# Moving x sums and Sinkhorn steps around the end of the first expert, in a fused attention and mixture-of-experts kernel

## The chip, the cores and the metric

The kernel runs on one core of a Trainium2 chip. The metric is the device time of one execution in microseconds. Shown are the median of several executions and one further execution taken with the hardware profiler, whose page and trace are quoted below. The engines are TensorE (PE: matmuls, with its weight loads listed as PEld), VectorE (DVE), ScalarE (ACT), GpSimd (POOL) and SyncE (SP), which here only issues DMAs.

## The reference

```python
# attention: batch 8, heads 8, seq 576, head_dim 64; result x is 4608 tokens x 512
q_p, k_p = phi(q), phi(k)                     # relu, times cos and sin of the position
x = (q_p @ (k_p.T @ v)) / (q_p @ sum(k_p) + 1e-6)
# mixture of experts: D = 512, E = 8 experts, F = 1024
P = exp(x @ w_gate - max)                     # 4608 x 8
for _ in range(8):                            # Sinkhorn
    P /= P.sum(1, keepdims=True) + 1e-9
    P /= P.sum(0, keepdims=True) + 1e-9
    P *= N / E
out = sum over e of P[:, e:e+1] * (relu(x @ w1[e]) @ w2[e])
```

The routing is dense: every token goes through every expert, and only the weights `P` depend on the Sinkhorn loop. `P` depends on all tokens, so it cannot be complete before the attention of the last batch is.

## The kernel before, in words

**First part, blocks 0 to 6.** A block is 512 tokens, and one loop turn per block has 16 slots. In slots 0 to 7 TensorE computes one of the eight 128-column pieces of expert 0's first layer (`ffn1`, four matmuls of 512 columns) and ScalarE applies the relu. In slots 8 to 15 it computes the second layer of the block's four 128-token tiles (`ffn2`), two slots a tile, and the tile is copied from PSUM into the accumulator `acc`. Between the slots the attention of the next batch is dealt out from a table (`at(block, slot, function)`). `xT` holds x with the feature on the partitions.

**Second part, blocks 7 and 8 and unit 0.** After block 6 the attention pools are given back and their memory is used again by `wB` (expert 1's weights), `H`, `S1/S2/S4`, `T...` and others. Blocks 7 and 8 are the last 1024 tokens of expert 0. Experts 1 to 7 are computed by a scheme of Strassen's kind with seven products in place of eight. It takes 384 tokens from the first half of all tokens and 384 from the second as a *unit*; there are six units an expert. A unit's first layer has four *groups* (`group`) of seven products, each of two matmuls of 384 columns. The products need sums of x parts, made by `x_sums(n, ts)`: four VectorE instructions, three into tiles `S1, S2, S4` and one in place in `xT`. The three are also saved to DRAM (`x_saved`), and later experts load them again (`x_again`). They also need sums of weights (`w1_steps`, sixteen VectorE instructions for one expert). The second layer is done by `Pair`, seven products of four matmuls of 256 columns for each pair of tiles; `stream` deals it into the fills of the next unit.

Each group calls `fill()` seven times. In unit 0 of expert 1 the fill is `start_fill`, in all later units `pair_fill`. Fill number k of unit 0 is therefore 7 x group + place. `start_fill` deals out the second layer of block 8 (`tiles`, from `dealt`) and steps of Sinkhorn.

**Sinkhorn** is the generator `sinkhorn()`, eight iterations of five steps: row sums and their reciprocal (`rs`, `rr`); the scaling and the column sums over a partition's tokens (`colp`); up to two weight steps; a TensorE matmul with ones that sums `colp` over the partitions into the bank `W2`, and the rest of the weight steps; the reciprocal of that and the second scaling of `P_tok`. `balanced(n)` takes n steps. Sinkhorn and the units meet on TensorE and VectorE only.

**Order.** `te, ve, se` (the tuple `bound`) are wrappers that add to each instruction an ordering dependency on the one before it on its engine, so that it runs in written order. From unit 1 on `ve` is the plain engine, and from expert 2 on `se` is, so that there the framework's scheduler chooses the order when the program is built. In the trace wrapped instructions have line 109, plain ones their own line. `gate(g)` multiplies a finished tile of expert 0 by its weight `P_tok[:, g, 0:1]`; two of the 36 go to GpSimd, and 34 to ScalarE, six a unit through units 1 to 5 and the last four in the first unit of expert 2.

Of the kernel before, what the change touches and what calls it, by code (L numbers as in the profile page):

```python
# [11 lines left out]
F16 = mybir.dt.float16  # L12

AX = mybir.AxisListType
ALU = mybir.AluOpType
# [10 lines left out]
def kernel(  # L26
# [10 lines left out]
    nc = tc.nc  # L37
# [117 lines left out]
    def ffn2(hT, w, c0, g, y_ps, fts):  # L155

        for ft in fts:
            te.matmul(
                out=y_ps,
                lhsT=hT[:, ft, c0 : c0 + P],  # L160
                rhs=w[1][:, ft, :],
                start=(ft == 0),
                stop=(ft == FT - 1),
            )
        if FT - 1 in fts:

            if g % 2 == 0 or g < (B - 1) * TCH // P:
                se.copy(out=acc(g), in_=y_ps)
            else:
                ve.tensor_copy(out=acc(g), in_=y_ps)  # L170

    def store(g, cols=slice(0, Dm), queues=(nc.sync, nc.sync)):
        for half, queue in enumerate(queues):
            w_ = 2 * g + half
            b, c = w_ // C, w_ % C
            rows = out[b * S : (b + 1) * S].rearrange("(p c) d -> p c d", c=C)
            queue.dma_start(
                out=rows[:, c, cols], in_=acc(g)[half * HP : (half + 1) * HP, cols]
            )

    with ExitStack() as p1:
        ld = p1.enter_context(tc.tile_pool(name="ld", bufs=4))
# [485 lines left out]
        for j in range(B):  # L668
# [82 lines left out]
            if j == 1:  # L751
                for name in "qkv":
                    for half in range(2):
                        at(j, 12, load, b + 2, half, name, True)
            elif j and b + 2 < B:
                for half in range(2):
                    at(j, 11 + half, load, b + 2, half, "qkv", True)
        y_pss = {}
        for j in range(B - 1):
            if j:  # L760
# [34 lines left out]

    NT = N // 2
    TU = 3 * P
    NU = NT // TU  # L800
    KH = KT // 2
    FH = FT // 2
    UG = TU // P
    DH = Dm // 2
    w_next = load_weights(wB, 1)

    H = hB.tile([P, 2, FT, 2 * TU], F16, name="H")
# [12 lines left out]
    Y = ps_k.tile([P, TCH], FP32, name="copied_ps")  # L820
    Z = ps_k.tile([P, TCH], FP32, name="p7_ps")

    def x_part(half, kh, n):
        t0 = half * NT + n * TU
        return xT[:, kh * KH : (kh + 1) * KH, t0 : t0 + TU]

    x_saved = dram.tile([NU, 3, P, KH * TU], F16, name="x_saved")

    def x_tiles():
        return [s2_pool.tile([P, KH, TU], F16, name=name) for name in ("S1", "S2", "S4")]  # L830

    def x_sums(n, ts):

        a11, a12, a21, a22 = (x_part(i, j, n) for i in range(2) for j in range(2))
        s1, s2, s4 = (t[:] for t in ts)
        for out_, in0, in1, op in (
            (s1, a21, a22, ALU.add), (s2, s1, a11, ALU.subtract),
            (s4, a12, s2, ALU.subtract), (a21, a11, a21, ALU.subtract),
        ):
            ve.tensor_tensor(out=out_, in0=in0, in1=in1, op=op)  # L840
            yield
        for i, t in enumerate(ts):
            nc.sync.dma_start(out=x_saved[n, i], in_=t[:].rearrange("p k t -> p (k t)"))
# [260 lines left out]
    def gate(g, pool=None):  # L1104

        if pool is None:
            se.mul(out=acc(g), in_=acc(g), mul=P_tok[:, g, 0:1])
# [43 lines left out]


    OFFSETS = {"P1": 0, "P2": 3, "P7": 4, "P6": 5, "P4": 8, "P5": 9, "P3": 13}
# [21 lines left out]
    def start_fill():  # L1175

        nonlocal k_fill
        if k_fill % 7 in (0, 2, 3, 5):
            next(tiles, None)
        if k_fill % 6 != 1:  # L1180
            balanced(1)
        k_fill += 1

    def pair_fill():
        nonlocal k_fill, slot2
        k_fill += 1
        if k_fill % 4 and stream and stream[0][0] <= slot2:
            _, pair, name = stream.pop(0)
            pair.step(name)
        if (k_fill % 7 == 6 or k_fill % 7 == 4 and k_fill % 4 in (1, 2)) and ungated:  # L1190

            gate(ungated.pop(0))
        slot2 += bool(k_fill % 4)

    mark(Y[:])
    for e in range(1, E):
# [3 lines left out]
        for n in range(NU):  # L1200
            hT = next_h()
            xs = xs_next
            for i in range(FH):
                group(hT, tws[i], xs, n, i, start_fill if e == 1 and n == 0 else pair_fill)
                m = (n + 1) % NU
                if e == 1 and m:

                    if n == 0:
                        xs_next = xs_first[1]
                        continue  # L1210
                    if i == 0:
                        xs_next = x_tiles()
                        sums_x = x_sums(m, xs_next)
                    next(sums_x)
                    if i == FH - 1:
                        next(sums_x, None)
                elif i == 1:
                    xs_next = x_tiles()
                    if not (e == E - 1 and m == 0):
                        x_again(m, xs_next)  # L1220
# [61 lines left out]
```

The softmax here doesn't subtract the row's maximum and nothing guards it: scores larger than these inputs give would overflow.

## Time and profile before

| what | value |
|---|---|
| median of 8 runs | 978.61 us (977.5 to 980.76) |
| the profiled execution | 978.05 us |
| its span, first to last instruction | 976.3 us |
| TensorE busy | 961.4 us, 98% of the span |
| VectorE busy | 807.5 us, 83% |
| ScalarE busy | 564.0 us, 58% |
| granted TensorE clock | 0.999 |

The rows of the timeline give start, duration, engine, line, operation and operands, and in brackets how long the engine sat idle before the instruction, with the engine that released it. A matmul row gathers several matmuls (x2 is one product of a group). The end of a matmul is modelled, and it overlaps the next one: the time that a product takes of TensorE is the distance from its start to the next start, 0.33 us for two matmuls of 384 columns and 0.22 us for one of 512. On VectorE and ScalarE too, the next instruction can start before the listed end of the one before.

The stretch that the change touches goes from block 6 (from 143.6 us) to the start of unit 1 (206.2 us). From there to the end TensorE works on units 1 to 41 of the seven experts, 18.3 to 18.6 us each.

### The profile page before, as it was taken

Reading aid. Unit: us, or ns where it says so; the run is one execution under the profiler, and the core shown is the slowest. Engines: PE = TensorE matmul, PEld = TensorE weight load, DVE = VectorE, ACT = ScalarE, POOL = GpSimd, SP = SyncE. Lnnn points to the kernel's source line nnn. Section 1 sums busy time; section 2 is a strip of 40 time slices with the busy share of each in tenths; the row PEclk is TensorE's granted clock in tenths of the full one; section 3 lists DMA queues with packets and bytes.
Section 4 is the critical chain, followed back from the end, with each engine's and each line's share of the span. In section 5 each row is a group of like instructions: output and inputs, shape, how many; then the busy total and the mean of one; then the engine's idle time right before and its main releaser. Section 6 shows DMA issues by size and latency. Waiting matters only on the chain.

```text
span 976.3 us, 20236 instructions
## 1 busy us (share of the span) xinstructions
PE 961.4 (98%) x7855; PEld 674.5 (69%) x7855; DVE 807.5 (83%) x1833; ACT 564.0 (58%) x1262; POOL 60.7 (6%) x82
## 2 busy tenths in 40 slices
PE   9999999999999999999999999999999999999997
PEld 6545555457777777777777777777777777777775
DVE  7767775888988987987888987988888888988887
ACT  5766665477776555555555555555555555555551
POOL 6231110010000000000000000000000000000001
PEclk9999999999999999999999999999999999999999
DMA  9999986330104401323103401323103401104435
GB/s 162 185 153 174 152 141 111 68 68 34 42 26 84 77 25 42 67 53 66 33 26 85 77 25 42 65 53 66 35 26 81 80 25 40 35 26 122 126 89 128
DMA packets 80336, 73.54 MB, mean 75 GB/s; under 512 B 33264, under 2 KB 72176, under 8 KB 80240
## 3 DMA queue, kind: packets, MB, share of 16 engines
q0 software_dynamic: 27232, 30.94, 20.4%
q1 hardware_dynamic: 52768, 41.06, 17.2%
q8 instruction: 61, 1.00, 0.4%
q14 instruction: 35, 0.29, 0.1%
q10 hardware_dynamic: 240, 0.26, 0.1%
HBM read 83.12 MB, written 12.98 MB: 98 GB/s over the span
## 4 chain that ended last, share of the span: by engine, by line
PE 88%; DMA 5%; DVE 3%; issue 2%; ACT 1%; POOL 1%; POOLq 0%; ACTq 0%; SPq 0%
PE rows_ps L109 33%; PE h_ps L109 26%; PE p_ps L109 11%; PE copied_ps L109 11%; PE y_ps L109 4%; PE small_ps L109 2%; DMA k_ld<-in_k_dram 1%; DMA w1e<-in_moe_w_dram 1%; DMA w2e<-in_moe_w_dram 1%; DMA acc_hi<-q_p 1%; DVE P_tok L109 1%; DVE colp L109 0%; POOL q_ld L202 0%; DVE rs L109 0%; DVE acc_hi L955 0%
## 5 line engine op out<-in xcount | busy, mean ns | idle before, releaser
L955 DVE SCALAR_TENSOR_TENSOR acc_lo<-rows_ps,P_tok,acc_lo 128x512 f32<-128x512 f32 (+1 forms) x322 | 203.1, 639 | 74.9 <-PE rows_ps L109 74.9
L109 PEld LDWEIGHTS <-H 128*128 128x128 f16 x2080 | 203.1, 98 | 82.5 <-issue 1.2
L891 ACT CAST u<-h_ps 128x384 f16<-128x384 f32 x288 | 137.8, 478 | 131.1 <-PE h_ps L109 131.1
L109 PEld LDWEIGHTS <-w1e 128*128 128x128 f16 x1632 | 157.7, 98 | 67.6 <-issue 5.2
L885 DVE CUSTOM_DVE_ANT_0 H<-p_ps,u 128x384 f16<-128x384 f32 x329 | 180.9, 550 | 6.6 <-PE p_ps L109 6.6
L109 PEld LDWEIGHTS <-hs 128*128 128x128 f16 x1500 | 146.6, 98 | 56.2
L109 PE MATMUL h_ps<-S,w1e 128*128 128x384 f16 x672 | 164.1, 326 | 0.7 <-ACT u L109 0.6
L109 PE MATMUL p_ps<-xT,T 128*128 128x384 f16 x672 | 164.1, 326 | 0.1
L109 PE MATMUL rows_ps<-V,H 128*128 128x256 f16 x1000 | 150.0, 273 | 0.7 <-DVE acc_hi L955 0.7
L109 PE MATMUL rows_ps<-w2e,hs 128*128 128x256 f16 x1000 | 150.0, 273 | 0.0
L109 PE MATMUL h_ps<-xT,w1e 128*128 128x384 f16 (+1 forms) x616 | 148.7, 350 | 0.1
L923 ACT ACTIVATE H<-h_ps 128x384 f16<-128x384 f32 x144 | 70.7, 491 | 95.0 <-PE h_ps L109 95.0
L109 PEld LDWEIGHTS <-T 128*128 128x128 f16 x1008 | 98.4, 98 | 30.1 <-issue 3.5
L109 PE MATMUL rows_ps<-w2e,H 128*128 128x256 f16 (+1 forms) x568 | 92.3, 285 | 0.0
L904 ACT COPY copied_ps<-h_ps 128x384 f32<-128x384 f32 x144 | 67.5, 469 | 35.4 <-PE h_ps L109 35.4
L914 ACT ACTIVATE H<-copied_ps 128x384 f16<-128x384 f32 x144 | 70.9, 492 | 20.3 <-PE copied_ps L109 20.3
L109 PE MATMUL h_ps<-S,T 128*128 128x384 f16 x336 | 81.8, 325 | 0.4 <-ACT copied_ps L109 0.3
L109 PE MATMUL copied_ps<-xT,w1e 128*128 128x384 f16 x336 | 82.1, 326 | 0.0
L109 PE MATMUL copied_ps<-w2e,H 128*128 128x256 f16 x504 | 75.5, 272 | 0.0
L109 PE MATMUL rows_ps<-V,hs 128*128 128x256 f16 x500 | 75.0, 272 | 0.0
L955 DVE SCALAR_TENSOR_TENSOR acc_lo<-copied_ps,P_tok,acc_lo 128x256 f32<-128x256 f32 x126 | 60.0, 476 | 0.6 <-PE copied_ps L109 0.2
L955 DVE SCALAR_TENSOR_TENSOR acc_hi<-rows_ps,P_tok,acc_hi 128x512 f32<-128x512 f32 (+1 forms) x56 | 41.2, 736 | 20.5 <-PE rows_ps L109 19.7
(145 smaller groups left out, 946.6 us busy)
## 6 DMA issues: line engine op xcount, KB each, us to landing
S<-x_saved SPq DMA_DIRECT2D x108, 192.0 KB, 2.4
out_dram<-acc_lo SPq DMA_DIRECT2D x62, 128.0 KB, 2.4
w1e<-in_moe_w_dram POOLq DMA_DIRECT2D x7, 1024.0 KB, 8.7
w2e<-in_moe_w_dram POOLq DMA_DIRECT2D x7, 1024.0 KB, 9.8
q_ld<-in_q_dram POOLq DMA_DIRECT2D x16, 288.0 KB, 6.6
k_ld<-in_k_dram POOLq DMA_DIRECT2D x16, 288.0 KB, 8.0
v_ld<-in_v_dram POOLq DMA_DIRECT2D x16, 288.0 KB, 9.2
x_saved<-S SPq DMA_DIRECT2D x18, 192.0 KB, 1.9
```

Of the source, the lines that this page charges most:

```text
L109: i = getattr(self.engine, name)(*args, **kwargs)
L885: latest = ve._custom_dve(TENSOR_ADD_SAT, out=out, in0=ps[:, 0:TU], in1=t[:], s0=FP32_MAX, s1=0.0)
L891: se.copy(out=t[:], in_=ps[:, 0:TU])
L904: se.copy(out=Y[:, 0:TU], in_=X[:, 0:TU])
L914: se.activation(out=h11, in_=Y[:, 0:TU], func=AF.Relu)
L923: se.activation(out=h12, in_=X[:, 0:TU], func=AF.Relu)
L955: ve.scalar_tensor_tensor(out=a, in0=rows, scalar=P_tok[:, g, self.e : self.e + 1], in1=a, op0=ALU.mult, op1=ALU.add,)
```

## The change

It has five parts.

1. The x sums of the first two units are made in block 6 (`at(B - 2, (2, 5)[n], x_sums_early, n)`: at the end of slots 2 and 5), into tiles of the attention's pools, saved to DRAM from there, and loaded into `S1, S2, S4` by six DMAs at the start of the second part. Before, they were made in slots 1 to 4 of block 7 and 0 to 3 of block 8.
2. In blocks 7 and 8 Sinkhorn is dealt from a table: 3 steps in slot 1, then 5 steps (a matmul, all that follows from it, up to the next `colp` and two weight steps) in slots 4, 8, 13, 17 and 22, counted from block 7 on. Before it was 3 steps, then alternately 1 and 4 in neighbouring slots, every five slots. The weight steps are spread 2, 3, 4, 3, 4 over iterations 0 to 4; before, four each over iterations 1 to 4.
3. In unit 0 the remaining 12 steps have their own fills (matmuls in fills 3, 12 and 21); before, nearly every fill took one step, the matmuls as they came.
4. Block 8's second layer is dealt in single matmuls, one a fill, with two in fills 1 and 15; before, two matmuls in four of seven fills. The last two matmuls go into the first fill of unit 1. The three banks are taken in another turn (`(i + 2) % 3`), and block 7's four copies out of PSUM are all ScalarE's; before, two of them were VectorE's.
5. `gate` always uses the wrapped ScalarE, also in expert 2.

No arithmetic is added or left out. What is new are six DMA loads of 192 KB.

```diff
-            if g % 2 == 0 or g < (B - 1) * TCH // P:
+            if g % 2 == 0 or g < B * TCH // P:
                 se.copy(out=acc(g), in_=y_ps)
...
+        def x_sums_early(n):
+            pool, name = ((kp_pool, "k_p"), (qp_pool, "q_p"))[n]
+            ts = [pool.tile([P, C, 2, D], F16, name=name) for _ in range(3)]
+            for _ in x_sums(n, [
+                t[:].rearrange("p c a d -> p (c a d)")[:, 0 : KH * TU].rearrange(
+                    "p (k t) -> p k t", k=KH
+                ) for t in ts
+            ]):
+                pass
+
+        for n in range(2):
+            at(B - 2, (2, 5)[n], x_sums_early, n)
...
-    def x_again(n, ts):
-        for i, t in enumerate(ts):
-            nc.sync.dma_start(out=t[:].rearrange("p k t -> p (k t)"), in_=x_saved[n, i])
+    def x_again(n, ts, earlier=None):
+        for i, t in enumerate(ts):
+            not_before(earlier, nc.sync.dma_start(
+                out=t[:].rearrange("p k t -> p (k t)"), in_=x_saved[n, i]
+            ))
...
-                    hT, w, c0, g, rows2[i % 3][:],
+                    hT, w, c0, g, rows2[(i + 2) % 3][:],
...
-            se.mul(out=acc(g), in_=acc(g), mul=P_tok[:, g, 0:1])
+            bound[2].mul(out=acc(g), in_=acc(g), mul=P_tok[:, g, 0:1])
...
-    tws, tw_steps = [], [[] for _ in range(8)]
+    tws, steps_left = [], []
     for i in range(FH):
-        tw, tw_steps[1 + i] = w1_steps(w_next, i)
+        tw, steps = w1_steps(w_next, i)
         tws.append(tw)
+        steps_left += steps
+    tw_steps = [[steps_left.pop(0) for _ in range(n)] for n in (2, 3, 4, 3, 4, 0, 0, 0)]
     xs_first = [x_tiles() for _ in range(2)]
     xs_next = xs_first[0]
-    sums_x = x_sums(0, xs_next)
+    for n in range(2):
+        x_again(n, xs_first[n], saved[-1])
...
-            2 if j < NJ - 1 else 4,
+            2 if j < NJ - 1 else 8,
...
-            if j == B - 1 and slot:
-                next(sums_x, None)
-            if j == NJ - 1:
-                if slot == 0:
-                    sums_x = x_sums(1, xs_first[1])
-                next(sums_x, None)
-            since = (j - B + 1) * NS + slot - 5
-            if since == -4:
-                balanced(3)
-            elif since >= 0 and since % 5 < 2:
-                balanced((1, 4)[since % 5])
+            balanced({1: 3, 4: 5, 8: 5, 13: 5, 17: 5, 22: 5}.get((j - B + 1) * NS + slot, 0))
...
     def start_fill():
...
-        if k_fill % 7 in (0, 2, 3, 5):
+        for _ in range(1 + (k_fill % 14 == 1)):
             next(tiles, None)
-        if k_fill % 6 != 1:
-            balanced(1)
+        balanced({3: 1, 4: 1, 6: 1, 8: 2, 12: 1, 13: 1, 15: 1, 17: 2, 21: 1, 22: 1}.get(k_fill, 0))
...
     def pair_fill():
...
+        for _ in range(2):
+            next(tiles, None)
...
                 k_fill = 0
-                for _ in tiles:
-                    pass
```

More of the change, by code (lines that the diff above doesn't have):

```diff
@@ L179, in store, with x_part, x_sums @@
             )
+    NT = N // 2
+    TU = 3 * P
+    NU = NT // TU
+    KH = KT // 2
+    FH = FT // 2
+    UG = TU // P
+    DH = Dm // 2
+    def x_part(half, kh, n):
+        t0 = half * NT + n * TU
+        return xT[:, kh * KH : (kh + 1) * KH, t0 : t0 + TU]
+    x_saved = dram.tile([NU, 3, P, KH * TU], F16, name="x_saved")
+    def x_sums(n, ts):
+        a11, a12, a21, a22 = (x_part(i, j, n) for i in range(2) for j in range(2))
+        s1, s2, s4 = ts
+        for out_, in0, in1, op in (
+            (s1, a21, a22, ALU.add), (s2, s1, a11, ALU.subtract),
+            (s4, a12, s2, ALU.subtract), (a21, a11, a21, ALU.subtract),
+        ):
+            ve.tensor_tensor(out=out_, in0=in0, in1=in1, op=op)
+            yield
+        for i, t in enumerate(ts):
+            saved.append(
+                nc.sync.dma_start(out=x_saved[n, i], in_=t.rearrange("p k t -> p (k t)"))
+            )
+    saved = []
     with ExitStack() as p1:
@@ L788 @@
     hs_pool = ctx.enter_context(tc.tile_pool(name="hs_pool", bufs=2))
[L798 to L804, printed above, removed]
     w_next = load_weights(wB, 1)
@@ L821 @@
     Z = ps_k.tile([P, TCH], FP32, name="p7_ps")
[L823 to L827, printed above, removed]
     def x_tiles():
         return [s2_pool.tile([P, KH, TU], F16, name=name) for name in ("S1", "S2", "S4")]
[L832 to L841, printed above, removed]
+    def x_again(n, ts, earlier=None):
         for i, t in enumerate(ts):
-            nc.sync.dma_start(out=x_saved[n, i], in_=t[:].rearrange("p k t -> p (k t)"))
-    def x_again(n, ts):
-        for i, t in enumerate(ts):
-            nc.sync.dma_start(out=t[:].rearrange("p k t -> p (k t)"), in_=x_saved[n, i])
+            not_before(earlier, nc.sync.dma_start(
+                out=t[:].rearrange("p k t -> p (k t)"), in_=x_saved[n, i]
+            ))
     def w1_sums(w, i):
@@ L1212 @@
                         xs_next = x_tiles()
-                        sums_x = x_sums(m, xs_next)
+                        sums_x = x_sums(m, [t[:] for t in xs_next])
                     next(sums_x)
```

## The prediction

> **What bounds the kernel now.** I read the page's engine table, then busy time by stage, then the timelines of TensorE, VectorE and ScalarE where a stage is not full.
>
> ```profile
> PE 961.4 (98%) x7855; PEld 674.5 (69%) x7855; DVE 807.5 (83%) x1833; ACT 564.0 (58%) x1262; POOL 60.7 (6%) x82
> ...
> 175.00:180.00 5.00, 4.97 (x25) 2.23 (x24) 4.76 (x14) 1.71 (x3) 0.00 (x0) 1.00 0.00 0
> 180.00:185.00 5.00, 5.00 (x25) 2.22 (x24) 4.79 (x13) 3.05 (x6) 0.00 (x0) 1.00 0.32 118
> 185.00:190.00 5.00, 3.81 (x22) 1.90 (x20) 4.69 (x14) 2.45 (x5) 0.76 (x1) 1.00 0.66 101
> 190.00:195.00 5.00, 4.58 (x25) 2.19 (x23) 3.68 (x10) 2.89 (x6) 0.00 (x0) 1.00 0.59 111
> 195.00:200.00 5.00, 3.69 (x20) 1.90 (x20) 4.63 (x10) 2.32 (x5) 0.00 (x0) 1.00 0.00 0
> 205.00:210.00 5.00, 4.14 (x25) 2.27 (x24) 4.96 (x11) 4.32 (x10) 1.63 (x2) 1.00 0.67 124
> ```
>
> Columns: stage, its length, then busy time (and instructions) of PE, PEld, DVE, ACT and POOL, granted clock, DMA share, GB/s. TensorE is the bound: from unit 1 on every unit takes 18.3 to 18.6 us, and its content is 56 x 0.1626 + 84 x 0.1089 = 18.25 us. Only unit 0 (185.06 to 206.03) has holes, and VectorE is full just before and in it.
>
> ```profile
> 187.17 0.39 PE L109 MATMUL copied_ps<-colp,ones_all 128*128 128x8 f32 x2 [1.19 <-DVE colp L109]
> 190.80 0.39 PE L109 MATMUL copied_ps<-colp,ones_all 128*128 128x8 f32 x2 [0.31 <-DVE colp L109]
> 195.63 0.39 PE L109 MATMUL copied_ps<-colp,ones_all 128*128 128x8 f32 x2 [0.74 <-DVE colp L109]
> 200.06 0.39 PE L109 MATMUL copied_ps<-colp,ones_all 128*128 128x8 f32 x2 [0.74 <-DVE colp L109]
> 205.71 0.49 PE L109 MATMUL h_ps<-S,w1e 128*128 128x384 f16 x2 [0.28 <-ACT u L109]
> 207.34 0.48 PE L109 MATMUL h_ps<-S,T 128*128 128x384 f16 x2 [0.28 <-ACT copied_ps L109]
> ...
> 184.33 0.20 DVE L109 RECIPROCAL t<-copied_ps 128x8 f32<-128x8 f32 x1
> 186.45 0.67 DVE L109 TENSOR_REDUCE colp<-P_tok 128x8 f32<-128x288 f32 x1
> ...
> 204.57 0.72 ACT L1107 ACTIVATE acc_lo<-acc_lo,P_tok 128x512 f32<-128x512 f32 x1
> 205.18 0.48 ACT L109 CAST u<-h_ps 128x384 f16<-128x384 f32 x1
> ```
>
> Four Sinkhorn matmuls wait for `colp`, and everything behind them on TensorE waits too. The brackets leave out about 0.16 us each, since matmul ends are modelled late; from start to start less content (0.33 a product, 0.43 two tile matmuls) the holes are 1.36, 0.48, 0.90 and 0.91, then 0.20 at 202.5 and 0.45 at 205.3: 4.3 us. The one at 205.71 comes from ScalarE: a line-1107 gate, one of the four written for expert 2, was put in front of a snapshot. Another 0.45 lies at 207.34, in unit 1. Two of 0.15 to 0.19 stand before the matmuls at 177.30 and 182.01, whose `colp` ends 0.05 earlier.
>
> **Blocks 7 and 8.** From 163.89 (slot 1) a slot is four matmuls, 0.865 us; a Sinkhorn matmul takes 0.24. The table's matmuls then stand at 167.35 (slot 4), 171.05, 175.61, 179.31 and 183.87. On VectorE an iteration runs from `t` to the end of `colp` in 2.80 us (168.52 to 171.32), and `t` starts 0.32 after its matmul (168.20 to 168.52). So the five `colp` behind these are ready at 170.47, 174.17, 178.73, 182.43 and 186.99, and the first, as before, at 166.41: 0.6 to 1.4 us ahead of each. The weight steps (0.25 each, up to four) fit before the next `t`. The waits of 0.15 and 0.19 go. The fifth matmul, 0.24, moves here from unit 0. Unit 0 starts at 185.20, 0.14 later than before.
>
> **The x sums.** Eight instructions of 0.55 us leave VectorE between 162 and 184. In block 6 they meet idle time: VectorE waits 1.93 us before `den` at 150.29 and 3.20 before `xT` at 155.96. The first four start behind `zsel` (end 148.36) and take about 2.1 (the last three from 166.33 to 167.9, and 0.55 for the first), so `den` starts 0.2 late; its `hl`, at 152.97 in place of 152.76, is used by TensorE at 153.17. The second four end at 155.1, before the 155.96. Cost nothing; without this cover up to 4.4 us.
>
> **DMAs.** Six saves leave SP from 149 to 155 in place of 162 to 184, and six loads of 192 KB (nearest row: later loads of the same tiles, 2.4 us to landing) stand behind them. SP has nothing else there: its transposes end by 141. Expert 1's weights, issued by GpSimd at 148.13 and 148.89, are in flight (9.6 and 13.6 us to landing, at about 205 GB/s, DMA engines full). The table asks VectorE for the first weight sum at 166.3, before at 171.24, and Sinkhorn stands behind it in order. The row: `w1e` lands at 157.7, 8.6 us ahead. The Trainium skill, "DMA: Bandwidth & Descriptors", section "Queues, rings and completion order", speaks against the move: each DMA engine takes turns between its queues, packet by packet. By that the saves, 1.18 MB, are served in between; as an estimate from the rate above, at most 1.18 MB / 205 GB/s = 5.8 us, so `w1e` lands by 163.5. By the row the step costs nothing, by the rule nothing with 2.8 us to spare. I take zero, and up to 2 us in the range. The saves also hold the memory that ScalarE writes as `H` from 163.58; at half rate the last lands near 159.
>
> **Copies.** Block 7's two VectorE copies (0.69 each) go to ScalarE at 0.59, which idles 1.1 to 3.0 us around each: nothing.
>
> **Unit 0.** Content: 27 products x 0.325 = 8.78, 30 tile matmuls x 0.216 = 6.48, three Sinkhorn matmuls 0.72: 15.98. Cover for the snapshots: a copy starts 0.52 after its product's start, lasts 0.47, and TensorE follows 0.06 later, 1.04 in all. Group 0 has 0.325 + 0.216 + 0.432 in between, 0.07 short; the others 1.08. In fill 6 ScalarE copies a tile (0.59) ahead of the next group's copy: about 0.33. Between the Sinkhorn matmuls of fills 3, 12 and 21 TensorE has nine products and nine or ten tile matmuls, 4.9 and 5.1 us, plus 0.24. VectorE has 0.32 + 2.80, two `add_relu` of 0.55 and, the second time, a tile copy of 0.68: 4.2 and 4.9. It fits, the second time by 0.4. The first of the three meets `colp` at 186.99 against 187.3. Unit 0 ends at 185.20 + 15.98 + 0.40 = 201.6 in place of 206.03: 4.4 saved.
>
> **Unit 1 and expert 2.** Two tile matmuls, 0.43, move into the first fill of unit 1, where TensorE has the hole of 0.45 before 207.34: nothing, and 0.43 if the hole has gone. The gates leave this stretch for expert 2's first unit. Six gates and the x sums together cost a unit of expert 1 18.62 - 18.28 = 0.34, so four cost at most 0.23 and at least nothing; I take 0.2.
>
> **Sum.** -4.4 + 0.2 = -4.2. Against the profiled execution: 978.05 - 4.2 = 973.8 (span 972.1, and 1.75 around it). The median is 0.56 above that execution: 974.4. If every hole named (4.3 + 0.34 + 0.45 = 5.1) closes, 973.5.
>
> **Rivals.**
> *The wait comes back* (0.13). VectorE remains the longest engine in blocks 7 and 8 and unit 0, and the table leaves 0.3 to 0.6 us at four matmuls. If an iteration takes 1.0 us longer than 2.80, the matmuls of slots 8 and 17 wait 0.4 each and those of fills 3, 12 and 21 wait 0.7, 0.1 and 0.6, 2.2 in all: -4.2 + 2.2, 976.6. Against it: nothing else is on VectorE then, and the chain is the same to 0.1 us in each iteration of before (2.79 from 184.33 to 187.12).
> *Weights or saves land late* (0.07). The rule above with a slower drain: VectorE stands before the first weight sum and the matmul of slot 8 waits about 2 us: 976.4.
> *The free order turns out worse* (0.10). From unit 1 VectorE's order, and from expert 2 ScalarE's, is laid out when the program is built, from what the builder thinks of the times before; this change alters those. If each of the 41 units waits 0.17 more, half of what the gates and x sums cost in expert 1, that is +7.0 - 4.2: 981.4. It decides from 0.10 a unit. For it: before, that order put four gates 100 us early. Against it: the later units of before come out at 18.28 to 18.56 with content 18.25, TensorE's order is written, and VectorE is idle 17% of the time.
> That a part does nothing is possible only for the gates: the order they are tied to starts where expert 2 does, so they can bunch there, at most 0.2 worse.
>
> **How the numbers follow.** The measurement of this kernel tells 0.2%, 2 us, from no change. The forecast case, 973.4 to 975.6, has 0.70. Of the returning wait 0.09 is faster by over 2 us and 0.04 within; of the late landing 0.04 and 0.03; of the free order 0.02 within and 0.08 slower. Faster 0.83, same 0.09, slower 0.08. The range reaches from 973.0 (all holes closed and half a microsecond for the median) to 977.0, which takes in the first two rivals' values.
>
> **What would show it.** Right: Sinkhorn's matmuls have no bracket with `colp`; unit 0 lasts 16.2 to 17 us instead of 21; VectorE shows the x sums between 148 and 155; no gate with a line of its own, and no gate of ScalarE in unit 0; units from 330 us on at 18.28. Wrong: a wait of VectorE for a DMA near 166; ScalarE's first `H` after 163.6; holes over 0.3 us before the fp32 matmuls; units over 18.4 us after expert 1.

## The result, and the profile after

The median after is 976.39 us (974.09 to 977.85), beside 978.75 for the kernel before in the same runs: the ratio is 0.9971, with a 95% interval of 0.9964 to 0.9979, so 2.1 to 3.5 us faster. The forecast of 974.4 was 2 us too low; the measured time lies inside the range that was given, 973.0 to 977.0. The profiled execution of the changed kernel took 975.94 us, its span 974.2 us at a granted clock of 1.0.

First the page's line of engine totals, then busy time by stage (columns as before: length, then PE, PEld, DVE, ACT, POOL, granted clock, DMA share, GB/s). This execution reaches block 7 1.19 us later than the one shown of before, 165.08 against 163.89 for its slot 1, so its stages lie that much later. Rows are cut at the marks `...`.

```profile
PE 960.0 (99%) x7855; PEld 675.2 (69%) x7855; DVE 807.3 (83%) x1831; ACT 565.4 (58%) x1264; POOL 60.7 (6%) x82
...
185.00:190.00 5.00, 5.00 (x29) 2.70 (x28) 3.98 (x10) 2.86 (x6) 0.76 (x1) 1.00 0.52 72
190.00:195.00 5.00, 4.52 (x28) 2.50 (x26) 3.27 (x8) 3.44 (x8) 0.00 (x0) 1.00 0.75 140
```

Unit 0 (185.83 to 202.19) is full but for one hole in 190 to 195, and VectorE has a second free there in every five. Two new holes stand where before had less or none: one in unit 1, one in the first unit of expert 2 (near 298). The timeline of TensorE shows all three, and the Sinkhorn matmuls of unit 0, now without a bracket:

```profile
187.95 0.28 PE L109 MATMUL copied_ps<-colp,ones_all 128*128 128x8 f32 x2
193.59 0.28 PE L109 MATMUL copied_ps<-colp,ones_all 128*128 128x8 f32 x2
198.81 0.28 PE L109 MATMUL copied_ps<-colp,ones_all 128*128 128x8 f32 x2
...
191.43 0.48 PE L109 MATMUL h_ps<-S,T 128*128 128x384 f16 x2 [0.48 <-ACT copied_ps L109]
207.79 0.48 PE L109 MATMUL p_ps<-xT,T 128*128 128x384 f16 x2 [0.85 <-DVE H L905]
298.59 0.48 PE L109 MATMUL h_ps<-S,w1e 128*128 128x384 f16 x2 [0.58 <-ACT u L911]
```

What stood ahead of that `H` is on the timeline of VectorE, in unit 1, where its order is free:

```profile
201.10 0.74 DVE L203 TENSOR_TENSOR S<-xT 128x768 f16<-128x768 f16 x1 [0.46 <-PE h_ps L109]
...
203.46 0.55 DVE L203 TENSOR_TENSOR S<-xT,S 128x768 f16<-128x768 f16 x1
203.92 0.68 DVE L170 COPY acc_hi<-rows_ps 128x512 f32<-128x512 f32 x1
204.53 0.54 DVE L905 CUSTOM_DVE_ANT_0 H<-p_ps,u 128x384 f16<-128x384 f32 x1
204.99 0.67 DVE L1007 TENSOR_TENSOR V<-w2e 128x1024 f16<-128x1024 f16 x1
205.59 0.41 DVE L990 TENSOR_TENSOR hs<-H 128x512 f16<-128x512 f16 x1
205.92 0.68 DVE L1008 TENSOR_TENSOR V<-V,w2e 128x1024 f16<-128x1024 f16 x1
206.53 0.41 DVE L990 TENSOR_TENSOR H<-H 128x512 f16<-128x512 f16 x1
206.86 0.41 DVE L990 TENSOR_TENSOR hs<-hs,H 128x512 f16<-128x512 f16 x1
207.20 0.54 DVE L905 CUSTOM_DVE_ANT_0 H<-p_ps,u 128x384 f16<-128x384 f32 x1
```

The product whose bank this `add_relu` (L905) empties began at 205.12, and its snapshot `u` was there at 205.65. It was VectorE that was late, by about 1.5 us. In the kernel before, the same work on VectorE lay like this:

```profile
204.71 0.56 DVE L840 TENSOR_TENSOR S<-xT 128x768 f16<-128x768 f16 x1 [1.48 <-PE h_ps L109]
...
207.44 0.55 DVE L885 CUSTOM_DVE_ANT_0 H<-p_ps,u 128x384 f16<-128x384 f32 x1
...
210.12 0.55 DVE L885 CUSTOM_DVE_ANT_0 H<-p_ps,u 128x384 f16<-128x384 f32 x1
...
213.52 0.55 DVE L840 TENSOR_TENSOR S<-xT,S 128x768 f16<-128x768 f16 x1
```

In neither trace does VectorE bring a backlog along: it idles until TensorE releases the first x sum of unit 2 (the brackets 1.48 and 0.46), and works without pause from there to the `H` of 210.12 and 207.20. Counted from TensorE's second product of unit 1, these instructions of VectorE start as follows:

| VectorE, us from that product | before (207.34) | after (203.50) | later by |
|---|---|---|---|
| first x sum of unit 2 | -2.63 | -2.40 | 0.23 |
| next `add_relu` (205.78, 202.34) | -1.56 | -1.16 | 0.40 |
| the `add_relu` behind it (207.44, 204.53) | +0.10 | +1.03 | 0.93 |
| the `add_relu` in question (210.12, 207.20) | +2.78 | +3.70 | 0.92 |

So three things made it late. TensorE comes from that release to its second product in 0.23 less, without its two holes of 0.45 and with other matmuls in part of their place. The first x sum takes 0.74 in place of 0.56 (0.17). And between the next two `add_relu` the builder has put the third x sum (0.46), which before ran 3.4 us behind the `H`; with the weight sum ahead of it a little longer, that makes 0.53. Between the last two `add_relu` the same five instructions lie in both traces. Before, this `H` came only 0.1 us late for TensorE (a product at 210.72 in place of 210.62), so there was no room for the 0.92.

Ahead of the snapshot of 298.59 the timeline of ScalarE shows three gates in a row (line 109: the wrapped engine, while all else there has lines of its own):

```profile
296.24 0.72 ACT L109 ACTIVATE acc_lo<-acc_lo,P_tok 128x512 f32<-128x512 f32 x1
296.86 0.71 ACT L109 ACTIVATE acc_hi<-acc_hi,P_tok 128x512 f32<-128x512 f32 x1
297.47 0.71 ACT L109 ACTIVATE acc_lo<-acc_lo,P_tok 128x512 f32<-128x512 f32 x1
298.08 0.46 ACT L911 CAST u<-h_ps 128x384 f16<-128x384 f32 x1
```

**Where the time went.** From slot 1 of block 7, cut at the same instructions in both traces (starts on TensorE; "to unit 1" runs from unit 0's last `mark` to the second product of unit 1, and each unit from that product to the next unit's):

| stretch, us | before | after | difference |
|---|---|---|---|
| blocks 7 and 8, from slot 1 | 21.17 | 20.75 | -0.42 |
| unit 0 | 20.97 | 16.36 | -4.61 |
| to unit 1 | 1.31 | 1.31 | 0 |
| unit 1 | 17.86 | 18.77 | +0.91 |
| units 2 to 5 | 74.49 | 74.49 | 0 |
| expert 2's first unit | 18.28 | 19.02 | +0.74 |
| 35 units behind it, and the end | 658.33 | 658.42 | +0.09 |
| from slot 1 to the end of the span | 812.41 | 809.12 | -3.29 |

So 5.03 us were gained up to unit 1, and 1.65 given back in two places behind it. The 1.19 us by which this execution came later to block 7 make -2.1 of the -3.29 in the two spans. They arise before 75 us, some 75 us ahead of anything that the change touches; half of them lie in block 2, where TensorE waits for a transposing DMA of the attention. Timelines of TensorE, before and after:

```profile
73.12 0.35 PE L109 MATMUL small_ps<-acc_hi,zsel 128*32 128x192 f16 x6 [0.70 <-DMA acc_hi<-q_p]
...
74.26 0.34 PE L109 MATMUL small_ps<-acc_hi,zsel 128*32 128x192 f16 x6 [1.26 <-DMA acc_hi<-q_p]
```

Here 1.14 of the 1.19 us are already there; block 6 itself takes 19.79 us in both. The kernels below reach slot 1 of block 7 anywhere from 163.18 to 170.44 us, and from the matmuls with `wg` in block 2 to those in block 7 all fourteen traces take 88.2 to 88.7 us. The last row of the table leaves this out, and is used for all the runs.

### The profile page after: what moved, and what is told of

It is laid out like the page before. It is cut to its first block, busy times and chain, and to the rows that moved or that the text cites. A ratio compares the mean times of both kernels' runs of the same rounds, so it can differ in the third digit from the quotient of the medians.

```text
span 974.2 us, 20258 instructions
## 1 busy us (share of the span) xinstructions
PE 960.0 (99%) x7855; PEld 675.2 (69%) x7855; DVE 807.3 (83%) x1831; ACT 565.4 (58%) x1264; POOL 60.7 (6%) x82
## 4 chain that ended last, share of the span: by engine, by line
PE 90%; DMA 5%; issue 2%; DVE 1%; POOL 1%; ACT 0%; POOLq 0%; DVEq 0%; SPq 0%; ACTq 0%
PE rows_ps L109 34%; PE h_ps L109 27%; PE p_ps L109 11%; PE copied_ps L109 11%; PE y_ps L109 4%; PE small_ps L109 2%; DMA k_ld<-in_k_dram 1%; DMA w1e<-in_moe_w_dram 1%; DMA w2e<-in_moe_w_dram 1%; DMA acc_hi<-q_p 1%; DVE acc_hi L975 0%; POOL q_ld L233 0%; POOL hs_last L990 0%; DMA out_dram<-acc_lo 0%; DVE H L905 0%
## 5 line engine op out<-in xcount | busy, mean ns | idle before, releaser
L905 DVE CUSTOM_DVE_ANT_0 H<-p_ps,u 128x384 f16<-128x384 f32 x329 | 180.9, 550 | 7.3 <-PE p_ps L109 7.2
L109 PE MATMUL rows_ps<-w2e,H 128*128 128x256 f16 (+1 forms) x568 | 94.4, 285 | 0.0
L975 DVE SCALAR_TENSOR_TENSOR acc_hi<-rows_ps,P_tok,acc_hi 128x512 f32<-128x512 f32 (+1 forms) x56 | 41.3, 737 | 20.6 <-PE rows_ps L109 19.8
```

Source lines behind the costliest of these rows:

```text
L109: i = getattr(self.engine, name)(*args, **kwargs)
L905: latest = ve._custom_dve(TENSOR_ADD_SAT, out=out, in0=ps[:, 0:TU], in1=t[:], s0=FP32_MAX, s1=0.0)
L975: ve.scalar_tensor_tensor(out=a, in0=rows, scalar=P_tok[:, g, self.e : self.e + 1], in1=a, op0=ALU.mult, op1=ALU.add,)
```

## The experiments

The question is which parts made the 5 us, and what the 1.65 are. One table of what was measured; each run follows with its edit. The last column is from slot 1 of block 7 to the end of the span.

| kernel | median, us | ratio to before (95%) | blocks 7, 8 | unit 0 | unit 1 | expert 2's first | slot 1 to end |
|---|---|---|---|---|---|---|---|
| e1_gates_only | 978.72 | 0.9992 (0.9981 to 1.0003) | 21.17 | 20.54 | 17.77 | 19.01 | 812.42 |
| e2_gates_free | 974.53 | 0.9957 (0.9942 to 0.9972) | 20.75 | 16.78 | 18.30 | 18.28 | 808.34 |
| e3_xsums_only | 977.08 | 0.9978 (0.9968 to 0.9989) | 20.91 | 19.26 | 17.86 | 18.27 | 810.66 |
| e4_tables_only | 975.05 | 0.9957 (0.9942 to 0.9972) | 21.16 | 17.63 | 18.30 | 18.27 | 809.53 |
| f1_gates_pool | 975.42 | 0.9960 (0.9945 to 0.9976) | 20.75 | 16.37 | 19.19 | 18.27 | 808.96 |
| f2_ve_written | 975.70 | 0.9967 (0.9954 to 0.9980) | 20.75 | 16.36 | 19.01 | 19.02 | 809.46 |
| f3_x2_early | 975.73 | 0.9975 (0.9965 to 0.9984) | 20.95 | 16.09 | 18.78 | 19.02 | 808.94 |
| f4_all | 977.75 | 0.9993 (0.9980 to 1.0006) | 20.88 | 16.09 | 20.72 | 18.28 | 810.12 |
| f5_x2_behind_h | 975.80 | 0.9974 (0.9963 to 0.9984) | 20.75 | 16.36 | 18.75 | 19.02 | 809.22 |
| f8_hs_too | 975.63 | 0.9957 (0.9942 to 0.9973) | 20.75 | 16.37 | 18.58 | 19.01 | 809.09 |
| f6_gates_spread | 974.84 | 0.9955 (0.9939 to 0.9971) | 20.75 | 16.37 | 18.77 | 18.28 | 808.49 |
| f9_hs_gates | 975.22 | 0.9957 (0.9940 to 0.9974) | 20.75 | 16.37 | 18.58 | 18.28 | 808.29 |

The intervals of the ratios are 0.2 to 0.3% wide, 2 to 3 us. Between these kernels they only tell the largest differences apart; the stretches of the traces tell the rest, where equal code repeats to about 0.02 us a unit.

**The parts alone.** e1 is the kernel before with the gates always on the wrapped ScalarE; e2 is the changed kernel with that undone.

```diff
 # e1: before
-            se.mul(out=acc(g), in_=acc(g), mul=P_tok[:, g, 0:1])
+            bound[2].mul(out=acc(g), in_=acc(g), mul=P_tok[:, g, 0:1])
 # e2: after
-            bound[2].mul(out=acc(g), in_=acc(g), mul=P_tok[:, g, 0:1])
+            se.mul(out=acc(g), in_=acc(g), mul=P_tok[:, g, 0:1])
```

> The kernel before with one line of the change: gate always on the wrapped ScalarE. Stages are taken between fixed matmuls of TensorE; before: slot 1 of block 7 to unit 0 21.17 us, unit 0 (first product to the mark in W2) 20.97, unit 1 (from the second product of its first group to that of unit 2) 17.86, expert 2's first unit 18.28. Theory (gates tied to the end of expert 1's order bunch at the start of expert 2): unit 0 shorter by the 0.45 hole at 205.7, expert 2's first unit 19.0, in all +0.3, about 979.0. Rival (the 0.74 lost in that unit after the change comes from another order there, not from the gates): that unit stays at 18.3, in all -0.5 to -0.9.

> The changed kernel with the gates as before (plain ScalarE in expert 2). Theory: expert 2's first unit returns from 19.02 to 18.3, and the four gates come into unit 0 or 1, where the first tile matmuls now cover more: unit 0 16.4 to 16.9. In all 0.2 to 0.7 faster than the changed kernel, 975.7 to 976.2. Rival (the gates in unit 0 cost what they cost before, 0.45 there and some in unit 1, where VectorE is late anyway): equal to the changed kernel or slower.

In e1 the gates leave unit 0, which falls by 0.43, and expert 2's first unit rises by 0.73 to 19.01: the theory holds in both stages, though its total of +0.3 does not (812.42 against 812.41 from slot 1 on). The timeline of TensorE in e1 has the same hole there as the changed kernel:

```profile
300.99 0.48 PE L109 MATMUL h_ps<-S,w1e 128*128 128x384 f16 x2 [0.58 <-ACT u L891]
```

In e2 that unit is back at 18.28, as its theory had it, and unit 0 and the stretch to unit 1 cost 0.63 more, of which unit 1 gives back 0.47. From slot 1 on, e2 is 0.78 us faster than the changed kernel, 0.58 of it in these stages: with the rest of the change in, the tie on the gates loses more than it brings.

e3 has the early x sums alone, with the tables, fills, copies and gates of before. e4 has the tables, fills and copies alone, with the x sums in blocks 7 and 8 as before and the gates as before.

```diff
 # e3: after (also as before: gates, copies, banks, and tile matmuls in the first fill of unit 1)
-            balanced({1: 3, 4: 5, 8: 5, 13: 5, 17: 5, 22: 5}.get((j - B + 1) * NS + slot, 0))
+            since = (j - B + 1) * NS + slot - 5
+            if since == -4:
+                balanced(3)
+            elif since >= 0 and since % 5 < 2:
+                balanced((1, 4)[since % 5])
...
-        for _ in range(1 + (k_fill % 14 == 1)):
+        if k_fill % 7 in (0, 2, 3, 5):
             next(tiles, None)
-        balanced({3: 1, 4: 1, 6: 1, 8: 2, 12: 1, 13: 1, 15: 1, 17: 2, 21: 1, 22: 1}.get(k_fill, 0))
+        if k_fill % 6 != 1:
+            balanced(1)
 # e4: after
-        for n in range(2):
-            at(B - 2, (2, 5)[n], x_sums_early, n)
...
-    for n in range(2):
-        x_again(n, xs_first[n], saved[-1])
+    sums_x = x_sums(0, [t[:] for t in xs_next])
...
+            if j == B - 1 and slot:
+                next(sums_x, None)
+            if j == NJ - 1:
+                if slot == 0:
+                    sums_x = x_sums(1, [t[:] for t in xs_first[1]])
+                next(sums_x, None)
```

> The kernel before with part 1 alone: the x sums of units 0 and 1 made in block 6, saved and loaded; Sinkhorn's slots, the dealing of block 8's second layer, the copies and the gates as before. Theory (the table brings the gain, the x sums only make room): the two waits of 0.15 to 0.19 in blocks 7 and 8 go and the first of unit 0 shrinks, since VectorE is 2.2 us less loaded in block 8; the waits of 0.9 in unit 0 stay, as no x sums lay there. Unit 0 20.0 to 20.6, 977.8 to 978.4. Rival (VectorE's load is the cause): unit 0 under 19, 976.5. Either way the prologue tells whether the 1.2 us by which block 7 started later after the change belongs to part 1.

> The changed kernel without part 1 and without the gates' change: x sums in blocks 7 and 8 as before, Sinkhorn by the table, block 8's second layer in single matmuls, copies on ScalarE. Theory: the x sums put 0.5 us a slot on VectorE for eight slots, 2.2 in each block, against 0.6 us to spare at slots 8 and 17: waits of up to 0.5 at two or three of the five matmuls, block 7 to unit 0 21.0 to 22.0, unit 0 16.4 to 17.0. 975.5 to 977. Rival (x sums needed): unit 0 also long, 977.5 or more.

The x sums alone bring 1.75 us, the tables and fills alone 2.88; e2, which has both, brings 4.07, so with the tables in, the x sums add 1.19. Neither text was right in its sizes: unit 0 of e3, at 19.26, lies between the theory's 20.0 to 20.6 and the rival's "under 19", and that of e4, at 17.63, lies over the theory's 16.4 to 17.0, while its blocks 7 and 8 (21.16) are in the range given. The timelines of TensorE tell which waits each takes. In e3 the first two waits for `colp` of before (1.19 and 0.31 by their brackets) are gone, and the other two (0.75 and 0.74) are left as they were:

```profile
195.11 0.39 PE L109 MATMUL copied_ps<-colp,ones_all 128*128 128x8 f32 x2 [0.75 <-DVE colp L109]
```

In e4 it is the other way round: the later ones are gone, and about half of the first remains. Unit 1 shows a wait for a snapshot of ScalarE:

```profile
187.79 0.39 PE L109 MATMUL copied_ps<-colp,ones_all 128*128 128x8 f32 x2 [0.58 <-DVE colp L109]
...
206.81 0.48 PE L109 MATMUL h_ps<-S,w1e 128*128 128x384 f16 x2 [0.83 <-ACT u L109]
```

So the x sums made VectorE late up to unit 0's start, and inside unit 0 the tables and fills ended the waits. Neither part does the other's work. That it was the dealing of Sinkhorn's steps follows from the brackets, which name `colp`; e4 also deals block 8's matmuls singly and changes the copies and the banks, and no run takes these apart.

**The last four gates.** f1 gives them to GpSimd. f6 keeps them on ScalarE, plain, each behind the snapshot written last before it.

```diff
 # f1: after
-            gate(ungated.pop(0))
+            gate(ungated.pop(0), nc.gpsimd if se is nc.scalar else None)
 # f6: after (cut: `latest_u` made known outside)
+        latest_u = se.copy(out=t[:], in_=ps[:, 0:TU])     # in snapshot
...
-            bound[2].mul(out=acc(g), in_=acc(g), mul=P_tok[:, g, 0:1])
+            i = se.mul(out=acc(g), in_=acc(g), mul=P_tok[:, g, 0:1])
+            if se is nc.scalar:
+                not_before(latest_u, i)
```

> The changed kernel, with the four gates that are left for expert 2 given to GpSimd instead of to ScalarE's written order. Theory (three bunched gates in front of the snapshot u at 298.08 hold TensorE up at 298.59): expert 2's first unit goes from 19.02 us back to about 18.3, everything earlier keeps its length, and the time is 0.7 us below the changed kernel's 976.4, near 975.7, ratio to the kernel before 0.9964. Rival (it is the scheduler's order of VectorE in that unit, not the gates, or GpSimd's gates slow VectorE beside them): the unit stays over 18.7 us, ratio 0.9971 or above.

> The changed kernel, with the last four gates as plain ScalarE instructions, each tied behind the snapshot u that was written last before it; in the order as built they lie singly between the copies of expert 2's first unit. Theory (the loss there is three gates in a row ahead of the snapshot at 298.08): expert 2's first unit goes from 19.02 back to 18.3 us, unit 1 stays at 18.77, 0.7 us below the changed kernel, ratio 0.9964. Rival (any gate in that unit costs): the unit stays over 18.6 us.

Both bring expert 2's first unit back to 18.3, so the row of gates was the cause. In f6 the gates lie singly on ScalarE (line 1129), and the stage has no hole on TensorE; from its timeline of ScalarE and its busy time by stage:

```profile
297.37 0.47 ACT L912 CAST u<-h_ps 128x384 f16<-128x384 f32 x1
297.73 0.73 ACT L1129 ACTIVATE acc_lo<-acc_lo,P_tok 128x512 f32<-128x512 f32 x1
...
294.00:299.00 5.00, 5.00 (x41) 3.76 (x39) 4.72 (x14) 3.52 (x9) 0.75 (x1) 1.00 0.78 153
```

f6's rival, that any gate there costs, falls. In f1 a part comes back elsewhere: GpSimd's order is free, the four gates ran as soon as `P_tok` was complete, in unit 1, and that unit rose from 18.77 to 19.19, against its text ("everything earlier keeps its length"). The run f4 below shows what GpSimd's gates do there.

**Unit 1.** Five runs are on the wait for `H`. f2 keeps VectorE in written order through unit 1; f3 makes unit 2's x sums in slot 0 of block 7, into a third set of tiles; f4 is f1, f2 and f3 together.

```diff
 # f2: after
+            if e == 1 and n == 1:                         # behind unit 1; before, behind unit 0
                 ve = nc.vector
 # f3: after
-    s2_pool = ctx.enter_context(tc.tile_pool(name="s2_pool", bufs=2))
+    s2_pool = ctx.enter_context(tc.tile_pool(name="s2_pool", bufs=3))
...
-    xs_first = [x_tiles() for _ in range(2)]
+    xs_first = [x_tiles() for _ in range(3)]
...
+            if j == B - 1 and slot == 0:
+                for _ in x_sums(2, [t[:] for t in xs_first[2]]):
+                    pass
...
-                    if n == 0:
-                        xs_next = xs_first[1]
+                    if n < 2:
+                        xs_next = xs_first[n + 1]
```

> The changed kernel, with VectorE kept in written order through unit 1 too and free only from unit 2 on. Theory (the free order puts unit 2's x sums, a weight sum and Pair's outputs ahead of the add_relu that TensorE waits for at 207.79): the wait of 0.85 us for that H goes, unit 1 lasts 17.9 to 18.2 us instead of 18.77, ratio 0.9965 (0.6 us below the changed kernel). Rival (VectorE is simply full there, 4.93 of 5 us, whatever the order): the wait is put elsewhere in unit 1 or into unit 2, units 1 and 2 together stay within 0.2 us of 37.4, ratio 0.9971. Second rival: the written order has the waits of its own that the free order avoids, and unit 1 comes out above 18.8.

> The changed kernel, with unit 2's x sums made at the start of block 7 (slot 0) into a third set of tiles, where VectorE has some 2.2 us idle between its last xT copy and Sinkhorn's first sums; four VectorE instructions of 0.55 us leave unit 1. Theory (unit 1's wait is VectorE's load): unit 1 falls from 18.77 to about 17.9 us, blocks 7 and 8 keep their 20.75, ratio 0.9963. Rival (it is the order, not the load): unit 1 stays over 18.5 us. Second rival: Sinkhorn's first colp comes later by up to 2 us and the matmul of slot 4 waits, blocks 7 and 8 at 21.5 to 22.5 us.

> The changed kernel with all three: the last four gates on GpSimd, VectorE in written order through unit 1, unit 2's x sums made in block 7. Theory (the two losses, 0.91 us in unit 1 and 0.74 us in expert 2's first unit, are what separates the changed kernel from the 5.0 us gained before): both go, 1.4 to 1.7 us below the changed kernel, near 974.8, ratio 0.9955. Rival (the losses move to later units): ratio 0.9968 or above.

All three theories fell. In f2 the wait is longer, not gone, as its second rival had it (unit 1 above 18.8: 19.01): the written order puts two `V` and the four instructions of the `hs` sums ahead of that `H` itself. Timeline of TensorE in f2:

```profile
210.79 0.48 PE L109 MATMUL p_ps<-xT,T 128*128 128x384 f16 x2 [1.09 <-DVE H L109]
```

f3 did not lighten unit 1 at all (18.78, over its rival's 18.5). Once unit 2's x sums were out of it, the builder's order pulled unit 3's into the same places, at the same 0.74, 0.56 and 0.54 us, and the wait stayed at 0.85; so f3 does not tell load from order. f4 is the worst of all, 2 us over the changed kernel in unit 1 itself, not in later units as its rival had it. Its timelines of GpSimd, VectorE and TensorE:

```profile
203.37 2.07 POOL L1129 TENSOR_SCALAR acc_hi<-acc_hi,P_tok 128x512 f32<-128x512 f32 x1
205.42 1.83 POOL L1129 TENSOR_SCALAR acc_lo<-acc_lo,P_tok 128x512 f32<-128x512 f32 x1
208.19 1.57 POOL L1129 TENSOR_SCALAR acc_hi<-acc_hi,P_tok 128x512 f32<-128x512 f32 x1
...
204.01 1.09 DVE L109 TENSOR_TENSOR V<-V,w2e 128x1024 f16<-128x1024 f16 x1
205.48 0.43 DVE L109 TENSOR_TENSOR H<-H 128x512 f16<-128x512 f16 x1
205.82 0.83 DVE L109 TENSOR_TENSOR hs<-hs,H 128x512 f16<-128x512 f16 x1
207.10 0.55 DVE L109 CUSTOM_DVE_ANT_0 H<-p_ps,u 128x384 f16<-128x384 f32 x1
...
207.70 0.48 PE L109 MATMUL p_ps<-xT,T 128*128 128x384 f16 x2 [2.80 <-DVE H L109]
```

Beside GpSimd's gates one `V` takes 1.09 us in place of 0.68 and one `hs` 0.83 in place of 0.41, and the gates that they meet take 2.07 and 1.83 in place of 1.57; the `add_relu` keeps its 0.55. Others are not slowed though they run inside a gate: the `H<-H` of 205.48 keeps its 0.43, an x sum at 203.54 its 0.55 and an `hs` at 205.03 its 0.41. The Trainium skill, "SBUF — State Buffer", section "SBUF: two separate sides", says of this pair that VectorE and GpSimd share one port pair, that an operation of VectorE with two SBUF inputs needs it against a GpSimd operation that reads SBUF, and that the one that comes second is fully blocked for the other's whole instruction. The rows agree in so far as only operations with two inputs from SBUF were slowed here. They do not agree that each is held for the other's length: at most one sum inside a gate was stretched by about 0.4, and the rest ran at their usual time. Which one it hits is not shown.

f5 and f8 go at what stands ahead of `H`. f5 ties unit 2's x sums behind it; f8 the first Pair's four `hs` as well; f9 is f8 with f6's gates.

```diff
 # f5: after
-            ve.tensor_tensor(out=out_, in0=in0, in1=in1, op=op)     # in x_sums
+            s = ve.tensor_tensor(out=out_, in0=in0, in1=in1, op=op)
+            if n == 2:
+                not_before(latest, s)
 # f8: f5, and in Pair
-                    self.sums()                           # in P1
+                    if not (self.e == 1 and self.first):
+                        self.sums()
...
+                if self.e == 1 and self.first:            # in P2
+                    self.sums(later=latest)
```

> The changed kernel, with unit 2's x sums tied behind the add_relu that TensorE waits for in unit 1 (the H at 207.20); VectorE's order is otherwise free. In the order as built, the three x sums leave the front, but a third sum V moves up into their place, so that H has the second V, an hs, the third V, an H and an hs (2.2 us) ahead of it. Theory (what matters is how much stands ahead of that H): VectorE has 0.6 less there than the 1.4 us of x sums suggest, the wait of 0.85 shrinks to between 0.3 and 0.6, unit 1 at 18.3 to 18.6. Rival (the x sums themselves are the cause): the wait goes, unit 1 at 17.9.

> As the run before, with the four sums hs of the first Pair of expert 1 tied behind the same add_relu as well. Theory (H stands behind work that TensorE needs later): the wait of 0.85 goes, the Pair's next matmuls find their hs in time, unit 1 lasts 17.8 to 18.0 us instead of 18.77, the rest as in the changed kernel: ratio to the kernel before 0.9962, 0.9 us below the changed kernel. Rival (VectorE is full there whatever stands first): the Pair's matmul on hs, 0.3 us behind H on TensorE, waits instead, unit 1 stays over 18.5 us.

> Both: unit 2's x sums and the first Pair's hs behind the add_relu, and the last four gates spread over expert 2's first unit. Theory: unit 1 at 17.9, expert 2's first unit at 18.3, everything else as in the changed kernel, 1.6 us below it, ratio to the kernel before 0.9955, and so the whole of the 5 us gained up to unit 1 kept. Rival (what is taken away there comes back in the units behind): ratio 0.9966 or above.

f5 moved nothing, neither as its theory nor as its rival had it: unit 1 at 18.75, the bracket 0.84 in place of 0.85. The x sums had gone, the third `V` had come up into their place, and the first `V`, now beside GpSimd's two gates, took 1.06. In f8 `H` is in time, and the wait has only moved 0.3 us down TensorE's order, to the Pair's matmul: that is the rival of its text. Timelines of VectorE and TensorE in f8:

```profile
203.46 1.06 DVE L1010 TENSOR_TENSOR V<-w2e 128x1024 f16<-128x1024 f16 x1
...
206.11 0.68 DVE L1021 TENSOR_TENSOR V<-w2e,V 128x1024 f16<-128x1024 f16 x1
206.72 0.54 DVE L907 CUSTOM_DVE_ANT_0 H<-p_ps,u 128x384 f16<-128x384 f32 x1
...
207.52 0.54 DVE L203 TENSOR_TENSOR S<-xT 128x768 f16<-128x768 f16 x1
207.99 0.41 DVE L992 TENSOR_TENSOR H<-H 128x512 f16<-128x512 f16 x1
...
208.45 0.61 PE L109 MATMUL rows_ps<-V,H 128*128 128x256 f16 x4 [0.65 <-DVE H L992]
```

From 202.27 to this last `H` VectorE has no pause. TensorE does not yet need all of it: the third `V` (0.61) and the x sum (0.47) could stand behind, and the first `V` is stretched by 0.38. But each time one thing was tied behind, the builder moved another up. What the runs show is that VectorE, without a pause, is behind TensorE at the start of the second layer by what lies ahead of the first instruction that TensorE needs, whichever that is; whether an order with only the needed ones in front would close the wait was not run, and stays open.

f9 has the shortest time from slot 1 on, 808.29, 0.83 below the changed kernel, with unit 1 at f8's 18.58 and not at the 17.9 of its text; f6 has 808.49 and e2 808.34. All three have ratios of 0.9955 to 0.9957, where the changed kernel has 0.9971. The ratios do not show that they are faster: the intervals overlap, and f8, as long as the changed kernel by its trace (809.09), has 0.9957 too. By the traces most of the difference is the one unit in expert 2.

## Why the prediction was right, and where it was off

**Faster, and by the waits named: right.** No Sinkhorn matmul has a bracket, unit 0 fell to 16.36 us, and e3 and e4 show both causes at work. By the traces the sum is -3.29 where the prediction had -4.2; the medians give -2.4. The gain up to unit 1 was larger than forecast by 0.6, the loss behind it by 1.5. That the median still fell into the range is in part luck: it lies outside the forecast case (973.4 to 975.6), close to the 976.4 and 976.6 of two rivals, neither of which happened.

**Blocks 7 and 8: the term was +0.14, measured -0.42.** The mis-sized quantity is the Sinkhorn matmul at 0.24 us, read from rows in which it had just waited. One that finds its input ready costs 0.14, from its start to the next. Timeline of TensorE, after:

```profile
168.53 0.28 PE L109 MATMUL copied_ps<-colp,ones_all 128*128 128x8 f32 x2
168.67 2.75 PE L109 MATMUL h_ps<-xT,w1e 128*128 128x512 f16 x12
```

Five of them make 0.5 us. The trace of before had two of this kind, at 168.20 and 172.65, each followed 0.14 later.

**Unit 0: the term was 16.38, measured 16.36, by two errors that cancel.** Three matmuls cost 0.3 less; the 0.07 in group 0 came as forecast (186.15 to 186.87 for three tile matmuls of 0.216). At fill 6 the hole is 0.64 (the bracket of 0.48 and 0.16) in place of 0.33. In f3, the same there but for one edit in block 7, it is 0.36, as forecast, and unit 0 takes 16.09. The difference is on ScalarE, at the `relu` ahead of the tile copy; timelines of the changed kernel and of f3:

```profile
190.03 0.49 ACT L109 ACTIVATE H<-h_ps 128x384 f16<-128x384 f32 x1 [0.94 <-PE rows_ps L109]
...
189.73 0.49 ACT L109 ACTIVATE H<-h_ps 128x384 f16<-128x384 f32 x1 [0.66 <-PE h_ps L109]
```

In the changed kernel the `relu` is released 0.3 later, by a tile matmul and not by its own product. Why it waits for that one is not shown.

**The two tile matmuls in unit 1's first fill: right.** The stretch to unit 1 is 1.31 in both; the hole took them.

**Unit 1: the term was 0, measured +0.91.** The prediction saw that VectorE's order is free from unit 1 on, but priced it as a rival over all 41 units, and otherwise let unit 1 keep the order and the cover of before. Of the 0.92 us by which `H` came late, 0.53 are the third x sum that the new order put ahead (with a weight sum a little longer), 0.17 a first x sum stretched to 0.74, and only 0.23 the time that TensorE no longer left. f5 and f8 show that taking what lay ahead away did not end the wait, since other sums came up. The prediction also says of all units from unit 1 on that they take 18.3 to 18.6 us; unit 1 itself took 17.86.

**The gates: the term was +0.2, "at most 0.23", measured +0.74.** The bound was worked out from units in which six gates are spread, and three in a row before a snapshot are another thing: 3 x 0.61 us of ScalarE, against a cover of about 1.04. That they can bunch was said; the bound beside it was wrong for just that case.

**The x sums in block 6: right.** They ran from 149.46 to 156.2, which is 148.27 to 155.0 on before's clock, and block 6 did not change its length.

**The DMAs: no cost on TensorE, as said, but with less to spare.** DMA issues in the changed kernel, from 145 to 170 us (KB each, median us to landing):

```profile
w1e<-in_moe_w_dram POOLq DMA_DIRECT2D x1, 1024.0 KB, 11.0
w2e<-in_moe_w_dram POOLq DMA_DIRECT2D x1, 1024.0 KB, 17.3
x_saved<-k_p SPq DMA_DIRECT2D x3, 192.0 KB, 8.7
x_saved<-q_p SPq DMA_DIRECT2D x3, 192.0 KB, 8.3
```

`w1e` came 1.4 us later than by the row (9.6), far from the 5.8 of the rule's bound; the estimate had let the saves share the 205 GB/s of loads, and reads and writes together moved 254 GB/s in 154 to 157 us. The saves took 8.3 to 8.7 us where the row had 1.9, so the last landed at 164.78, on before's clock 163.6 and some 5 us behind the 159 of the estimate. ScalarE's first `H` met that:

```profile
164.96 0.60 ACT L109 ACTIVATE H<-h_ps 128x512 f16<-128x512 f32 x1 [0.46 <-DMA x_saved<-q_p]
```

It came some 0.2 us late, which the prediction had named as a sign of being wrong, and TensorE shows no hole: the cover of 4.6 us (159 to 163.58) was just used up.

**The rivals.** The returning wait is refuted by the brackets that are gone, the late landing by the row above. The free order over all units is refuted too: from the second product of expert 2's second unit to that of the last unit, TensorE takes 623.03 us before and 623.02 after. Orders that the builder laid out did cost time in two units: the 0.74 of the gates, and more than half of the 0.91 of unit 1.

**The rest of the difference.** By the traces 975.5 would follow for the median (978.75 - 3.29); measured was 976.39. The interval of the ratio takes in 975.5. The traces give the early DMAs no part in this 0.9 us: the delay ahead of block 7 arose before 75 us, and they are issued from 150 us on. The other runs point the same way. The median less the time from slot 1 on is 166.3 for before and for e1; for the eleven kernels with the early x sums it is 166.2 to 167.6, in the middle 166.5, and the changed kernel's own 167.3 is one of the highest. What made it so is not shown.

## What to carry to other kernels

When a stall is taken out, price the first stage behind it anew: the engines there lose the slack that the stall gave them, and where the builder lays out their order, it may put other work ahead; here 0.9 of 5 us went that way, a quarter by slack and more than half by order. A tie between moved instructions, with the rest of their engine left free, lets them land as one block in front of something urgent; tie each to its neighbour instead (0.7 us for four gates). Measure such effects between the same two instructions of two traces, since the time at which an execution reaches the stage can differ by more than the effect.

## What the runs showed of the hardware

A save of 192 KB that shares the DMA engines with weight loads of 1 MB took 8.3 to 8.7 us to landing, against 1.9 with no weight load in flight (medians of three each), while the loads lost only 1.4 and 3.7 us (11.0 for 9.6, 17.3 for 13.6). A small fp32 matmul after a wait takes TensorE 0.24 us, without one 0.14. Of the fp16 sums of VectorE that ran beside a gate of GpSimd some were stretched by about 0.4 us (0.68 to 1.09, 0.41 to 0.83) and the gate with them (1.57 to 1.83 and 2.07), while others kept their time (0.41, 0.43, 0.55).
